# Token-major keys through DRAM instead of TensorE, a partial sum read by ScalarE, and weight pieces dealt anew, in an attention and MLP kernel

## The chip, the cores and the metric

One core of one Trainium2 chip. The metric is the device time of one execution in microseconds (us); all data are float32. Where several runs of a kernel exist, the median of its fast runs is quoted.

## The reference, cut to what matters

```python
def _attn_ref(q, k, v, f_logit):              # batch 4, 8 heads, 768 tokens, head size 48
    f = 1.0 / (1.0 + np.exp(-f_logit))
    for t in range(S):
        state = f[:, :, t, :, None] * state + np.einsum('bhd,bhe->bhde', k[:, :, t], v[:, :, t])
        y[:, :, t] = np.einsum('bhd,bhde->bhe', q[:, :, t], state)

def _moe_ref(x, w_in, w_out):                 # x: (3072, 384), d_ff = 2048
    h = x @ w_in
    g = h * (1.0 / (1.0 + np.exp(-1.702 * h)))
    return g @ w_out
```

The output y of the recurrence, transposed to (3072, 384), is the x of the MLP.

## The kernel before

The sequence is cut into 12 units of 256 tokens. In each unit the recurrence is done in six levels of blocks: masked scores of decayed keys and queries (`sc`), their products with v (`y`), then the products of keys and v that give the new states (also a bank named `sc`, told apart by its line: L523 before, L552 after), then the part of y that comes from the states of before (`inter`). Feature-major q, k and f come from VectorE's 32x32 block transposes; units 0 to 2 use TensorE for that. The MLP of earlier units is dealt in small portions between these parts, so that TensorE has something to do while the other engines prepare the next part. Weights arrive packed and are converted piece by piece in units 0 to 3.

The state products need the keys token-major (`kn`). They are turned on TensorE:

```python
        def turn_k(a0):
            if a0 == 0:
                t["kn"] = att.tile([P, NP, NG, P], F32, tag="kn", name=f"kn_{n}", bufs=1)
            pt = ps.tile([P, 2, NG, P], F32, tag="mm", name=f"tkn_{n}_{a0}", bufs=4)
            for a in range(2):
                for g in range(NG):
                    x = (a0 + a) * U + g * G
                    nc.tensor.transpose(pt[:, a, g, :], X[:, 1, x:x + G], ident)
            nc.scalar.copy(t["kn"][:, a0:a0 + 2], pt)

        for a0 in (0, 2):
            part("T")(lambda a0=a0: turn_k(a0))
```

Order of the parts, and the share of the MLP that is dealt behind each:

```python
            else:                                   # next unit's turning, units 3 and later
                kind, states = parts.pop()
                parts += [("B", begin_k), (kind, lambda: (states(), begin_gates()))]
                parts.insert(i - 3, ("B", lambda: (begin_f(), begin())))
    # ... cut ...
    def steady(kind):
        return {"W": 3, "V": 4, "S": 3, "T": 1, "B": 1, "K": 1}.get(kind, 0)
    # ... cut ... the fifth argument is the number of weight pieces converted in the unit
    merge(0, fill, 0, steady, 8)
    fill += mlp_blocks((0, 0)) + mlp_blocks((0, 1))
    merge(1, fill, UNIT // 2 - LAG // 2, steady, 10, hold=1)
    # ... cut ...
    merge(2, fill, UNIT, steady, 8)
    # ... cut ...
    merge(3, fill, 3 * UNIT // 2 - LAG // 2, steady, 6, by=0.7)
```

The second MLP product of units 3 and later is done with seven half-size products in banks X, W, Y and Z, some of which are read and then go on accumulating. Y's first reader was on VectorE:

```python
        def p6():
            nc.vector.tensor_tensor(row("u2"), t["p1"], t["Y"], ALU.add)
        def p3():
            nc.vector.tensor_tensor(out_(0)[:, HC:], t["u2"], t["Z"], ALU.add)
            store(n, 0, out_(0))
```

Of the kernel before, what the change touches and what calls it, by code (L numbers as in the profile page):

```python
# [9 lines left out]
F32 = mybir.dt.float32  # L10
# [3 lines left out]
ALU = mybir.AluOpType  # L14
# [9 lines left out]
def kernel(  # L24
# [33 lines left out]
    nc = tc.nc  # L58
    B, H, S, D = q.shape
    DM = H * D  # L60
    DFF = moe_w_in.shape[1]
    P = 128
    C = 64
    G = 128
    U = 256
    NG = U // G
    NC = U // C
    NU = S // U
    NP = H // 2
# [3 lines left out]
    NK = DM // P  # L73
    NFF = DFF // P
    FG = 4
    PAIRS_AHEAD = 3
    N_FILL = 3
    N_TURN = 2
    NA = NP * U
    NALL = B * NU  # L80
    assert S % U == 0 and NALL % 2 == 0 and NL == 6 and NG == 2 and DM % P == 0 and D <= HS

    const = ctx.enter_context(tc.tile_pool(name="const", bufs=1))
    ld = ctx.enter_context(tc.tile_pool(name="ld", bufs=1))
    att = ctx.enter_context(tc.tile_pool(name="att", bufs=1))
    wp = ctx.enter_context(tc.tile_pool(name="wp", bufs=2))
    mlp = ctx.enter_context(tc.tile_pool(name="mlp", bufs=2))
# [44 lines left out]
    X = const.tile([P, 3, NX], F32, name="X")  # L132
# [6 lines left out]

    w_in = const.tile([P, NK, DFF], F32, name="w_in")  # L140
    w_out = const.tile([P, NFF, DM], F32, name="w_out")
    v_toks = [tc.dram_tile([U, DM], F32, name=f"v_tok{j}") for j in range(2)]
    D2, DR = 2 * D, P - 2 * D
    assert NP == NK + 1 and NK * DR == D2
# [5 lines left out]
    for r in range(NGR):  # L150
        ffs = range(r * FG, (r + 1) * FG)
        for ff in ffs[::2]:
            f = slice(ff * P, (ff + 2) * P)
# [159 lines left out]
    def attention(n):  # L313
# [5 lines left out]
        t = {"tms": [F]}  # L319
        parts = []  # L320

        def part(kind):
            return lambda fn: parts.append((kind, fn))
# [174 lines left out]
# [7 lines that stand above are left out]
                    nc.tensor.transpose(pt[:, a, g, :], X[:, 1, x:x + G], ident)  # L505
            nc.scalar.copy(t["kn"][:, a0:a0 + 2], pt)

        for a0 in (0, 2):
            part("T")(lambda a0=a0: turn_k(a0))

        @part("S")
        def _():
# [139 lines left out]
    def mlp_o7(n, g):  # L652
        a = lambda i, j: lambda f: g[j * 2 + f // FG][:, f % FG, i * G:(i + 1) * G]
        s = lambda i: lambda f: g["S", f // FG][:, f % FG, i * G:(i + 1) * G]
        b = lambda i, j: lambda f: quarter(w_out, i, j)[:, f]
        T_ = lambda i: lambda f: T[i][:, f] if i < 4 else T[4](f)
        t = {}

        def out_(tt):
            if "o" not in g:  # L660
                g["o"] = mlp.tile([P, U // P, DM], F32, tag="osb", name=f"osb_{n}", bufs=1)
            return g["o"][:, tt]

        def row(name):
            t[name] = mlp.tile([P, HC], F32, tag=name, name=f"{name}_{n}", bufs=1)
            return t[name]

        def p1():
            nc.scalar.copy(row("p1"), t["X"])

        def p4():
            nc.scalar.copy(row("p4"), t["W"])

        def p2():
            nc.scalar.copy(out_(0)[:, :HC], t["X"])
            last_sum(n, g)

        def p6():
            nc.vector.tensor_tensor(row("u2"), t["p1"], t["Y"], ALU.add)  # L679

        def p5():
            nc.scalar.copy(row("p5"), t["Z"])

        def p7():
            nc.vector.tensor_tensor(row("u3"), t["p1"], t["Y"], ALU.add)
            nc.vector.tensor_tensor(out_(1)[:, :HC], t["u3"], t["p4"], ALU.subtract)
            nc.vector.tensor_tensor(out_(1)[:, HC:], t["u3"], t["p5"], ALU.add)
            store(n, 1, out_(1))

        def p3():  # L690
            nc.vector.tensor_tensor(out_(0)[:, HC:], t["u2"], t["Z"], ALU.add)
            store(n, 0, out_(0))


        products = (
            ("X", a(0, 0), b(0, 0), p1, True), ("W", a(1, 1), T_(4), p4, True), ("X", a(0, 1), b(1, 0), p2, False),
            ("Y", s(0), T_(2), p6, True), ("Z", a(1, 0), T_(1), p5, True), ("Y", s(1), T_(3), p7, False),
            ("Z", a(0, 1), b(1, 1), p3, False),
        )

        def one(bank, lhs, rhs, done, new, f):
            if new and f == 0:
                t[bank] = ps.tile([P, HC], F32, tag="mm", name=f"o_{n}_{bank}", bufs=4)
            nc.tensor.matmul(  # L704
                t[bank], lhsT=lhs(f), rhs=rhs(f), start=(new and f == 0), stop=(f == HF - 1), skip_group_check=True,
            )
            if f == HF - 1:
                done()
        return [(HC, lambda p=p, f=f: one(*p, f), 0) for p in products for f in range(HF)]
# [104 lines left out]
    def parts_of(n):  # L814

        parts = list(units[n][1])
        _, inter = parts.pop()
        if n:
            kind, scores = parts[0]
            _, ahead = units[n - 1][1][-1]  # L820
            parts[0] = kind, lambda: (ahead(), scores())
        if n < N_TURN:

            def with_v(l):
                kind, fn = parts[l]
                return kind, lambda: (fn(), load_vl(n, l) if n == 0 or l else None, keep_up(2 * (n == 0 and l < 3)))
            parts[:NL] = [with_v(l) for l in range(NL)]
        if n + 1 < NALL:
            begin_f, begin, begin_k, begin_gates = units[n + 1][0]
            i = len(parts)  # L830
            if n + 1 < N_FILL:

                parts.append(("K", lambda: (begin_k(), begin_gates(), load_vl(n + 1, 0) if n + 1 < N_TURN else None)))
                parts.insert(i - 4, ("B", begin if n == 0 else lambda: None))
                parts.insert(i - 5, ("B", begin_f))
                if n:

                    kind, head = parts[0]
                    parts[0] = kind, lambda: (head(), begin())
            else:  # L840
                kind, states = parts.pop()
                parts += [("B", begin_k), (kind, lambda: (states(), begin_gates()))]
                parts.insert(i - 3, ("B", lambda: (begin_f(), begin())))
        else:
            parts.append(("W", inter))
        return parts

    def merge(n, fill, columns, share, pieces=0, hold=0, by=1.0, chores=()):



        parts = parts_of(n)
        total = sum(share(kind) for kind, _ in parts)
        converting = {"W": 3, "T": 3, "B": 1} if n < N_FILL - 1 else {"W": 3, "V": 4, "S": 3, "T": 1, "B": 1}
        total_ops = sum(converting.get(kind, 0) for kind, _ in parts)
        held = sum(share(kind) for kind, _ in parts[:hold])
        at = at_ops = done = ops = 0
        for kind, fn in parts:
            ready = state["done"]
            fn()  # L860
            for chore in chores[:2]:
                chore()
            chores = chores[2:]
            at += share(kind)
            at_ops += converting.get(kind, 0)
            n_ops = min(int(pieces * NOP * at_ops / (by * total_ops)), pieces * NOP) - ops
            ops += n_ops
            first, n_columns = done, max(0, columns * (at - held) / (total - held) - done)

            def some(end):  # L870
                nonlocal done
                while fill and done < end and fill[0][2] <= ready:
                    w, emit, _ = fill.pop(0)
                    emit()
                    done += w
            for i in range(n_ops):
                some(first + n_columns * i / n_ops)
                convert()
            some(first + n_columns)

    def steady(kind):
        return {"W": 3, "V": 4, "S": 3, "T": 1, "B": 1, "K": 1}.get(kind, 0)

    UNIT = NFF * NK * U + U // P * NFF * DM

    for j in range(3):
# [10 lines left out]
        load_raw(1, j)  # L897
    load_vn(1)
    fill = []
    merge(0, fill, 0, steady, 8)  # L900
    fill += mlp_blocks((0, 0)) + mlp_blocks((0, 1))
    merge(1, fill, UNIT // 2 - LAG // 2, steady, 10, hold=1)
    fill += mlp_blocks((1, 0), (1, 1)) + mlp_blocks((0, 2), (1, 2))
    merge(2, fill, UNIT, steady, 8)
    fill += mlp_blocks((2, 0), (2, 1)) + mlp_blocks((2, 2), (0, 3)) + mlp_blocks((1, 3), (2, 3))
    merge(3, fill, 3 * UNIT // 2 - LAG // 2, steady, 6, by=0.7)
    fill_order.close()
    for n in range(3, NALL):
        fill += mlp_unit(n)
    for n in range(4, NALL):  # L910
        merge(n, fill, NFF * NK * U + 7 * HF * HC, steady, chores=list(sums_of_b()) if n == 4 else ())
    for _, emit, _ in fill:
        emit()

# [28 lines left out]
```

## Time and profile before

| | before |
|---|---|
| time, median of 3 runs | 658.35 us (655.55 to 660.19) |
| profiled span and its mean clock | 653.7 us, 1.000 |
| a late unit (5 to 10) | 48.71 us |
| first product of the MLP (`h`) | 51.82 us |
| first scores of unit 4 | 210.19 us |

The last line is used below as the mark between the **front** (units 0 to 3, where weights are converted) and the **late** part. The lines of the profile are in the prediction. In the rows of tenths each digit is one fortieth of the span and 9 means 90% or more. In the tables of groups and waits the name after `L` is the source line; lines of the kernel after are 2 to 31 higher.

### The profile page before, as it was taken

Reading aid. Unit: us, or ns where it says so; the run is one execution under the profiler, and the core shown is the slowest. Engines: PE = TensorE matmul, PEld = TensorE weight load, DVE = VectorE, ACT = ScalarE, POOL = GpSimd, SP = SyncE. Lnnn points to the kernel's source line nnn. Section 1 sums busy time; section 2 is a strip of 40 time slices with the busy share of each in tenths; the row PEclk is TensorE's granted clock in tenths of the full one; section 3 lists DMA queues with packets and bytes.
Section 4 is the critical chain, followed back from the end, with each engine's and each line's share of the span. In section 5 each row is a group of like instructions: output and inputs, shape, how many; then the busy total and the mean of one; then the engine's idle time right before and its main releaser. Section 6 shows DMA issues by size and latency. Waiting matters only on the chain.

```text
span 653.7 us, 20397 instructions
## 1 busy us (share of the span) xinstructions
PE 632.3 (97%) x8958; PEld 542.0 (83%) x8958; DVE 444.7 (68%) x802; ACT 229.7 (35%) x477; POOL 60.2 (9%) x116
## 2 busy tenths in 40 slices
PE   6979989999999999999999999999999999999997
PEld 5656767767778789989989989989989889989997
DVE  2998978788787658558558558558559557553571
ACT  3565444333224324324324324324334333232120
POOL 3050020010001002002002002002002002000000
PEclk9999999999999999999999999999999999999999
DMA  8898874384044634614605615605604202101000
GB/s 186 211 221 216 216 157 126 99 207 79 25 91 123 167 74 121 164 29 119 167 25 127 160 27 128 159 26 129 159 27 107 64 25 64 38 2 26 25 1 24
DMA packets 67554, 67.67 MB, mean 104 GB/s; under 512 B 30410, under 2 KB 61290, under 8 KB 67466
## 3 DMA queue, kind: packets, MB, share of 16 engines
q1 hardware_dynamic: 67466, 66.38, 40.5%
q8 instruction: 70, 1.15, 0.7%
q14 instruction: 18, 0.15, 0.1%
HBM read 56.92 MB, written 8.65 MB: 100 GB/s over the span
## 4 chain that ended last, share of the span: by engine, by line
PE 85%; DVE 8%; DMA 3%; ACT 2%; issue 1%; SPq 1%; DVEq 0%; ACTq 0%
PE h L727 37%; PE o_X L704 7%; PE o L755 7%; PE o_Y L704 7%; PE o_Z L704 7%; PE sc L384 5%; PE y L448 4%; PE o_W L704 4%; PE t L339 2%; PE y L563 2%; PE sc L523 1%; PE tkn L505 1%; DMA bits<-in_moe_w_in_dram 1%; DMA xT<-yT 1%; DVE X L439 1%
## 5 line engine op out<-in xcount | busy, mean ns | idle before, releaser
L727 PE MATMUL h<-xT,w_in 128*128 128x256 f32 (+1 forms) x1152 | 259.8, 381 | 5.7 <-DMA xT<-yT 3.0
L727 PEld LDWEIGHTS h<-xT,w_in 128*128 128x128 f32 x1152 | 215.3, 190 | 39.1 <-issue 3.8
L733 DVE TENSOR_TENSOR g<-h,sg 128x256 f32<-128x256 f32 (+1 forms) x192 | 80.8, 422 | 98.2 <-ACT sg L732 95.7
L732 ACT ACTIVATE sg<-h 128x256 f32<-128x256 f32 (+1 forms) x192 | 73.2, 383 | 193.1 <-PE h L727 186.9
L423 ACT COPY Kc<-X 128x512 f32<-128x512 f32 x69 | 46.2, 669 | 118.1 <-DVE X L439 84.7
L755 PE MATMUL o<-w_out,g 128*128 128x384 f32 x192 | 66.1, 493 | 0.0
L439 DVE TENSOR_TENSOR X<-X,tot 128x1024 f32<-128x1024 f32 x45 | 55.1, 1224 | 15.4 <-PE sc L384 10.2
L755 PEld LDWEIGHTS o<-w_out,g 128*128 128x128 f32 x192 | 35.3, 190 | 22.9 <-issue 1.4
L704 PE MATMUL o_X<-w_out,g 128*128 128x192 f32 x288 | 51.9, 329 | 0.0
L704 PE MATMUL o_Y<-T,S 128*128 128x192 f32 x288 | 51.1, 331 | 0.1
L704 PEld LDWEIGHTS o_Y<-T,S 128*128 128x128 f32 x288 | 46.5, 190 | 2.6 <-DVE u L679 1.2
L704 PEld LDWEIGHTS o_X<-w_out,g 128*128 128x128 f32 x288 | 47.3, 190 | 0.9
L410 DVE TENSOR_TENSOR A<-sc,masks 128x512 f32<-128x512 f32 x72 | 46.8, 679 | 0.0
L376 POOL TENSOR_TENSOR tot<-F 128x512 f32<-128x512 f32 x12 | 12.5, 1040 | 342.2 <-DVE st L540 342.2
L448 PE MATMUL y<-A,vl 64*48 64x64 f32 x2304 | 41.2, 217 | 0.4 <-issue 0.3
L448 PEld LDWEIGHTS y<-A,vl 64*48 64x48 f32 x2304 | 36.2, 120 | 3.9 <-issue 3.6
L327 DVE STREAM_TRANSPOSE X<-raw 128x1024 f32<-128x1024 f32 x18 | 36.7, 2040 | 2.5 <-PE y L563 2.2
L571 ACT COPY yT<-y 48x512 f32<-48x512 f32 x48 | 27.8, 580 | 13.0 <-PE y L563 12.4
L384 PEld LDWEIGHTS sc<-X,Kc 48*64 48x64 f32 x1344 | 24.0, 134 | 8.2 <-issue 3.4
L384 PE MATMUL sc<-X,Kc 48*64 48x64 f32 x1344 | 28.3, 220 | 1.8 <-DVE A L410 1.0
L376 POOL TENSOR_TENSOR tot<-tot 128x256 f32<-128x256 f32 (+4 forms) x60 | 27.4, 457 | 4.7
L704 PE MATMUL o_Z<-w_out,g 128*128 128x192 f32 x144 | 26.6, 331 | 0.0
(93 smaller groups left out, 662.5 us busy)
## 6 DMA issues: line engine op xcount, KB each, us to landing
vl<-v_tok SPq DMA_DIRECT2D x60, 192.0 KB, 2.9
bits<-in_moe_w_out_dram SPq DMA_DIRECT2D x8, 768.0 KB, 10.4
bits<-in_moe_w_in_dram SPq DMA_DIRECT2D x8, 576.0 KB, 7.0
v_tok<-in_v_dram SPq DMA_DIRECT2D x10, 384.0 KB, 4.2
vn<-v_tok SPq DMA_DIRECT2D x10, 384.0 KB, 6.9
xT<-yT SPq DMA_DIRECT2D x24, 144.0 KB, 2.8
raw<-in_q_dram SPq DMA_DIRECT2D x18, 192.0 KB, 4.0
raw<-in_f_logit_dram SPq DMA_DIRECT2D x18, 192.0 KB, 4.8
```

The costliest lines, as they stand in the source:

```text
L327: nc.vector.transpose(out.rearrange("p (a i j) -> p a j i", a=NP, j=R), raw[:, j].rearrange("p a (j d) -> p (a j) d", j=R)[:, :, :32],)
L376: nc.gpsimd.tensor_tensor(tn, t2[:, :, 0], t2[:, :, 1], ALU.mult)
L384: nc.tensor.matmul(out[g * HS:(g + 1) * HS, h, a, :], lhsT=lhs(h, a * U + g * G), rhs=rhs(h, a * U + g * G), start=True, stop=True,)
L410: nc.vector.tensor_tensor(A[:, :, c:c + w].rearrange("p h (x t) -> p h x t", t=64), t["sc"][:, :, c:c + w].rearrange("p h (x t) -> p h x t ...
L423: nc.scalar.copy(c.rearrange("p (n m) -> p n m", m=m), X[:, j, :NA].rearrange("p (n two m) -> p n two m", two=2, m=m)[:, :, hf, :],)
L439: nc.vector.tensor_tensor(qk, qk, by, ALU.mult)
L448: nc.tensor.matmul(dst(h, g, a), lhsT=vls[n, u][g * 64:(g + 1) * 64, (2 * a + h) * D:(2 * a + h + 1) * D], rhs=A(h, g, a), start=(start an ...
L704: nc.tensor.matmul(t[bank], lhsT=lhs(f), rhs=rhs(f), start=(new and f == 0), stop=(f == HF - 1), skip_group_check=True,)
L727: nc.tensor.matmul(ph, lhsT=w_in[:, c, ff * P:(ff + 1) * P], rhs=xTs[n][:, c, :], start=(c == 0), stop=(c == NK - 1))
L732: nc.scalar.activation(sg, ph, AF.Sigmoid, scale=1.702)
L733: nc.vector.tensor_tensor(g[ff // FG][:, ff % FG, :], ph, sg, ALU.mult)
L755: nc.tensor.matmul(t["po"], lhsT=g[ff // FG][:, ff % FG, tt * P:(tt + 1) * P], rhs=w_out[:, ff, :], start=(ff == ffs[0]), stop=(ff == ffs[ ...
```

## The change

Its intent: take the key transposes off TensorE, which has no gap in a late unit, and let VectorE (32x32 blocks) and a store to and fetch from DRAM (the blocks) do them for seven units, 4 to 10; put more MLP between the last scores and the states so that this detour has time; take next k behind the states; let ScalarE read the sum Y that goes on; and deal the weight pieces 6, 10, 9, 7 instead of 8, 10, 8, 6, with three `o` products' columns moved from unit 1 to unit 2.

```diff
+    CARRY = range(N_FILL + 1, NALL - 1)
...
+    k_toks = [tc.dram_tile([NG, G, P // 32, 32 * NP], F32, name=f"k_tok{j}") for j in range(2)]
...
-        for a0 in (0, 2):
-            part("T")(lambda a0=a0: turn_k(a0))
+        def carry_k(g):
+            nb = G // 32
+            z = mlp.tile([P, nb, 32, NP], F32, tag="sum", name=f"z_{n}_{g}", bufs=3)
+            nc.vector.transpose(
+                z.rearrange("p b d a -> p a b d"),
+                X[:, 1, :NA].rearrange("p (a g b t) -> p g a b t", a=NP, g=NG, b=nb)[:, g],
+            )
+            for i in range(P // 32):
+                nc.sync.dma_start(
+                    out=k_toks[n % 2][g, :, i].rearrange("(b t) x -> t b x", t=32),
+                    in_=z[i * 32:(i + 1) * 32].rearrange("p b d a -> p b (d a)"),
+                )
+
+        def fetch_k(g):
+            if g == 0:
+                t["kn"] = att.tile([P, NP, NG, P], F32, tag="kn", name=f"kn_{n}", bufs=1)
+            z = mlp.tile([P, P, NP], F32, tag="sum", name=f"kt_{n}_{g}", bufs=3)
+            nc.sync.dma_start(out=z.rearrange("p d a -> p (d a)"), in_=k_toks[n % 2][g].rearrange("t i x -> t (i x)"))
+            nc.scalar.copy(t["kn"][:, :, g, :], z.rearrange("p d a -> p a d"))
+
+        if n not in CARRY:
+            for a0 in (0, 2):
+                part("T")(lambda a0=a0: turn_k(a0))
+        else:
+            parts[-1] = "V3", parts[-1][1]
+            part("C")(lambda: (carry_k(0), fetch_k(0)))
+            part("C2")(lambda: (carry_k(1), fetch_k(1)))
...
         def p6():
-            nc.vector.tensor_tensor(row("u2"), t["p1"], t["Y"], ALU.add)
+            nc.scalar.copy(row("p6"), t["Y"])
...
-            nc.vector.tensor_tensor(out_(0)[:, HC:], t["u2"], t["Z"], ALU.add)
+            nc.vector.tensor_tensor(out_(0)[:, HC:], t["p1"], t["Z"], ALU.add)
+            nc.vector.tensor_tensor(out_(0)[:, HC:], out_(0)[:, HC:], t["p6"], ALU.add)
...
-                parts += [("B", begin_k), (kind, lambda: (states(), begin_gates()))]
-                parts.insert(i - 3, ("B", lambda: (begin_f(), begin())))
+                if n in CARRY:
+                    parts += [("B", begin_f), ("B2", begin), ("S1", lambda: (states(), begin_gates())), ("K3", begin_k)]
+                else:
+                    (as before)
...
+    def late(kind):
+        return {"V": 6, "V3": 3, "C": 2, "C2": 4, "S1": 3, "S": 5, "B": 3, "B2": 4, "K3": 3, "T": 2, "W": 5}.get(kind, 0)
...
-    merge(0, fill, 0, steady, 8)
+    merge(0, fill, 0, steady, 6)
-    merge(1, fill, UNIT // 2 - LAG // 2, steady, 10, hold=1)
+    merge(1, fill, UNIT // 2 - LAG // 2 - 3 * DM, steady, 10, hold=1)
-    merge(2, fill, UNIT, steady, 8)
+    merge(2, fill, UNIT + 3 * DM, steady, 9)
-    merge(3, fill, 3 * UNIT // 2 - LAG // 2, steady, 6, by=0.7)
+    merge(3, fill, 3 * UNIT // 2 - LAG // 2, steady, 7, by=0.7)
...
-        merge(n, fill, NFF * NK * U + 7 * HF * HC, steady, chores=...)
+        merge(n, fill, NFF * NK * U + 7 * HF * HC, late, chores=...)
```

More of the change, by code (lines that the diff above doesn't have):

```diff
@@ L841, in parts_of @@
                 kind, states = parts.pop()
-                parts += [("B", begin_k), (kind, lambda: (states(), begin_gates()))]
-                parts.insert(i - 3, ("B", lambda: (begin_f(), begin())))
+                if n in CARRY:
+                    parts += [("B", begin_f), ("B2", begin), ("S1", lambda: (states(), begin_gates())), ("K3", begin_k)]
+                else:
+                    parts += [("B", begin_k), (kind, lambda: (states(), begin_gates()))]
+                    parts.insert(i - 3, ("B", lambda: (begin_f(), begin())))
         else:
@@ L910 @@
     for n in range(4, NALL):
-        merge(n, fill, NFF * NK * U + 7 * HF * HC, steady, chores=list(sums_of_b()) if n == 4 else ())
+        merge(n, fill, NFF * NK * U + 7 * HF * HC, late, chores=list(sums_of_b()) if n == 4 else ())
     for _, emit, _ in fill:
```

## The prediction

> **What bounds the kernel now.** I read the page's busy totals and slices first, then busy time by stretch, the chain over one late unit, the groups, the waits and the DMA issues.
>
> From the page of the kernel before: busy totals, and the slices of TensorE, VectorE and DMA.
>
> ```profile
> PE 632.3 (97%) x8958; PEld 542.0 (83%) x8958; DVE 444.7 (68%) x802; ACT 229.7 (35%) x477; POOL 60.2 (9%) x116
> PE   6979989999999999999999999999999999999997
> DVE  2998978788787658558558558558559557553571
> DMA  8898874384044634614605615605604202101000
> ```
>
> TensorE is full from the fourth slice (49 us) on, with only small dents; VectorE and DMA are full only in the first five slices. So there are two stages with two bounds. Busy time by stretch shows them: columns are length, then busy time and count of TensorE, weight load, VectorE, ScalarE and GpSimd, then clock, DMA share and GB/s.
>
> ```profile
> 20.00:50.00 30.00, 24.82 (x677) 18.56 (x677) 28.72 (x65) 18.95 (x35) 10.24 (x10) 1.00 0.82 203
> 125.00:160.00 35.00, 31.37 (x450) 22.65 (x449) 30.95 (x55) 13.25 (x27) 3.75 (x8) 1.00 0.64 139
> 317.06:365.87 48.81, 48.78 (x732) 44.67 (x735) 32.76 (x53) 17.34 (x36) 4.83 (x8) 1.00 0.40 101
> 463.22:511.98 48.76, 48.76 (x732) 44.66 (x735) 32.73 (x53) 17.28 (x36) 4.58 (x8) 1.00 0.34 86
> ```
>
> In 20 to 50 us VectorE works 28.72 of 30 us: it is the bound of unit 0. A late unit lasts 48.8 us and TensorE has no gap in it; VectorE (33 us), ScalarE (17 us) and DMA (40%) all have room. There only less TensorE work, or a smaller wait inside it, makes the time shorter. The chain of the late unit shows what its time is made of (start, length, what):
>
> ```profile
> 376.48 1.09 PE sc L384 x64
> 378.47 10.56 PE h L727 x48
> 389.03 0.44 PE tkn L505 x4
> 389.46 2.59 PE h L727 x12
> 392.06 0.44 PE tkn L505 x4
> 396.78 0.92 PE sc L523 x64
> 405.73 2.80 PE o_Y L704 x16
> 411.12 2.84 PE o_Y L704 x16
> ```
>
> The key transposes (L505) take 0.44 us twice in each unit and stand squarely between products of h; they are the work that the change takes from TensorE. The second o_Y chain takes 2.84 us where 16 such products take 2.60 elsewhere.
>
> [...] So the state products L523 that wait for the keys would hold everything behind them. The trace agrees: in unit 0, L523 waited 1.3 us for the copy of the keys, and nothing behind it started meanwhile. [...] The existing 128x1024 block transposes (L327) take 2.04 us. [...] the trace's 192 KB stores land after 1.9 us[...].
>
> **The change part by part.** First the groups and issues that give the costs (mean ns of one after the comma; for DMA, KB and median us to landing).
>
> ```profile
> L327 DVE STREAM_TRANSPOSE X<-raw 128x1024 f32<-128x1024 f32 x18 | 36.7, 2040 | 2.5 <-PE y L563 2.2 <-DMA vl<-v_tok 0.2
> L506 ACT COPY kn<-tkn 128x512 f32<-128x512 f32 x24 | 14.0, 584 | 2.7 <-PE tkn L505 1.9
> L423 ACT COPY Kc<-X 128x512 f32<-128x512 f32 x69 | 46.2, 669 | 118.1 <-DVE X L439 84.7
> PEld o_Y L704 <- DVE u L679: 1.2, 4, 0.3
> vl<-v_tok SPq DMA_DIRECT2D x60, 192.0 KB, 2.9
> vn<-v_tok SPq DMA_DIRECT2D x10, 384.0 KB, 6.9
> out_dram<-osb SPq DMA_DIRECT2D x18, 192.0 KB, 1.9
> ```
>
> *1. Key transposes leave TensorE.* Seven units (4 to 10) x 2 x 0.44 us = 6.2 us, all on the path, since TensorE has no gap there. In their place, each unit gets two VectorE transposes of 128x512: half of 2.04 us each, so 2.0 us; VectorE goes to about 35 of 48 us, beside the path. ScalarE's two copies stay, reading SBUF instead of PSUM: 2 x (0.669 - 0.584) = 0.17 us. DMA gets eight stores of 64 KB and two fetches of 256 KB: 1 MB more beside some 5 MB, at 40% share. None of it is on the path by its amount.
>
> *2. The latency of the detour.* It counts only if it outlasts the MLP put between the last scores and the states. My estimate for half 0: block transpose 1.0, four issues at about 0.5 = 2.0, store landing 2 to 3, issue 0.6, fetch 3 to 4, copy 0.7: 9 to 11 us. Half 1 ends about 1 to 2 us later if its stores are issued ahead of the first fetch, and about 5 to 6 us later if they queue behind it. The keys are final some 3 us after those scores start (in the trace 376.41 and about 379), so kn is ready 13 to 21 us after them. The room: a unit deals 23,040 columns in about 39 us; the new shares are 6+6+3+2+4+3+4+3+3 = 34, and 3+2+4+3+4 = 16 of them lie between V3 and the states: 39 x 16/34 = 18.4 us, plus about 3 us of scores and sums around them: 21 us. It fits, in the worst case only just. Before, the states (396.60) came 20 us after the scores as well.
>
> *3. ScalarE reads the going o_Y.* The wait in the second o_Y and the odd 0.2 us before it come from a busy VectorE queue. A 0.31 us copy on ScalarE ends the wait sooner. The o_Y products take 5.44 to 5.67 us a unit where 5.40 is free of it; nine units give about 1.2 us. VectorE gets one 0.35 us addition more per unit off the path, but at the very end of the kernel it is on it: +0.35 us.
>
> *4. Pieces 8, 10, 8, 6 become 6, 10, 9, 7.* One weight piece costs VectorE five instructions (0.55 + 0.55 + 0.35 + 0.55 + 0.35 = 2.35 us). Two fewer in unit 0, where VectorE is the bound from 14 to 42 us: -4.7 us at most, and I count -4.4 because levels also wait on scores and copies. Nothing is paid back in unit 1 (still ten), and unit 2 has the room (VectorE 22.05 of 32 us in 93 to 125). Unit 3 begins in the stretch 125 to 160, VectorE 30.95 of 35, with 3.6 us of TensorE gaps: another piece there may cost 1 us of its 2.35.
>
> *5. 3 x 384 columns moved from unit 1 to unit 2.* They are 1,152 x 1.7 ns = 1.95 us of MLP. Before, TensorE idles some 1.8 us (91.2 to 93.0) until xT has landed; this work fills that. I count -1.5 us.
>
> *Sum:* -6.2 - 1.2 + 0.35 - 4.4 + 1.0 - 1.5 = -12.0 us. Against it +1.5 us, about 0.2 us a late unit, for new small waits of tighter places (V1 and V2 get 6.9 us of MLP instead of 8.2, and next k comes behind the states). Net -10.5: 658.35 becomes about 648, 1.6% less.
>
> **The rivals.**
> *A: the states wait for the detour.* For it: half 1 may be as late as the room is long[...]. Against: that queue stands idle from about 380 to 395 us, where the new stores fall. With 1 us lost in each of seven units the kernel would be at 653 to 655; with 2 us lost at about 660, no gain.
> *B: the front gives nothing.* If DMA (82 to 89% in the first 80 us) and not VectorE times unit 0, or unit 3 pays the pieces back, only parts 1 and 3 remain: some 653. For it: ScalarE's conversions waited 3.4 us for weights. Against: one weight pair fewer is due by then, and VectorE never stops in that stretch.
> *C: VectorE's and ScalarE's queues turn against TensorE.* Block transposes of 1 us and next k's work behind the states may delay g or the next scores; k's chain (2.0 transpose, 1.3 copies, 1.2 product, 0.7 copy) is over 5 us against 3.4 + 3.4 us of MLP and 1 us of y. If program order held, up to 1 us a unit: 654. Against: in the trace next F, q and k are taken as soon as their buffers are free, and early freeing of the keys by the block transposes only helps that.
> *D: all goes well,* waits vanish and the front gives 6 us: 644 to 645, right at 2%.
>
> **Range and chances.** The removed work (6.2 us) is nearly sure; the front (0 to -6) and new waits (0 to +7) carry the spread. That gives 642.5 to 655.5. A gain over 2% (under 645.2) asks for D; I give it 0.26. Over 2% slower asks for waits of some 3 us a unit: 0.03. The rest is within 2%.
>
> **What would show it.** Right: no tkn between h products in the late units but for unit 3 and the last; a late unit of 47.6 to 47.9 us; L523 without a wait on kn; o_Y at 5.4 us a unit; first h at about 47.4 instead of 51.8 us; no gap ahead of unit 2's h. Wrong: waits of L523 on the copy of kn of over 0.5 us a unit (A), first h still at 50 us or later, or larger gaps from 125 to 160 us (B), new waits of scores on Kc or of h on g (C).

The queue in rival A is SPq, which issues the DMAs. Its longest waits in the kernel before on TensorE and VectorE were 16.6 us (on the y products, L448) and 15.8 us (on g, L733).

## The result, and the profile after

| | before, same rounds | after |
|---|---|---|
| median of 4 fast runs | 657.59 us (655.55 to 660.19) | 649.62 us (647.16 to 651.03) |
| profiled span, mean clock | 653.7 us, 1.000 | 649.2 us, 0.991 |
| late unit (mean of four) | 48.71 us | 47.63 us |
| first `h` | 51.82 us | 49.86 us |
| first scores of unit 4 | 210.19 us | 210.97 us |
| moved by DMA | 67.67 MB | 75.03 MB |

The ratio is 0.9873 (95%: 0.9823 to 0.9922), 1.3% faster, which at a threshold of 2% counts as the same. A ratio is the mean time of one kernel's fast runs over the mean of the other's in the same rounds, so it is not quite the ratio of the medians. The profiled run of the kernel after was the slowest of its four (651.03 us), that of the kernel before one of the fastest (655.66 us), so the two profiles differ by 4.5 us only.

The late units did what was asked. Busy time by stretch, kernel after (same columns as in the prediction), for the first and the last of four late units in a row:

```profile
315.00:362.63 47.63, 47.63 (x725) 43.86 (x727) 34.66 (x54) 18.15 (x37) 4.29 (x8) 1.00 0.52 130
457.88:505.51 47.63, 47.63 (x725) 43.86 (x728) 34.66 (x54) 18.12 (x37) 4.30 (x8) 1.00 0.38 103
```

TensorE is still full, with less to do; VectorE rose to 34.66 us as worked out (35). The chain of waits over one late unit, kernel after (start, length, what):

```profile
373.95 18.33 PE h L757 x84
...
393.32 0.92 PE sc L552 x64
...
404.41 2.60 PE o_Y L734 x16
...
409.61 0.65 PE o_Y L734 x4
...
412.25 2.15 PE o_Y L734 x12
```

Where `h` was broken twice by `tkn`, it now runs through, and the states follow without a wait. The second o_Y takes 0.65 + 2.15 = 2.80 us here in two pieces round the scores, and the first 2.60: 5.40 a unit. The 0.20 us above 2.60 is no wait for VectorE: in these chains the first large products right behind scores or y products take 0.20 us longer, whatever they are (twelve o_Y 2.15 instead of 1.95 us, sixteen o_X behind the states' products 2.80). The detour itself, in the timeline of the kernel after (start, length; SPq is the queue that issues the DMAs):

```profile
375.46 1.11 DVE L515 STREAM_TRANSPOSE z<-X 128x512 f32<-128x512 f32 x1
...
376.60 2.95 SPq L520 DMA_DIRECT2D k_tok<-z  x4
...
388.71 1.14 ACT L530 COPY kn<-kt 128x512 f32<-128x512 f32 x1
...
393.13 1.10 PE L552 MATMUL sc<-vn,kn 64*64 64x48 f32 x64
```

From the first block transpose to the last copy of `kn` (389.85) it is 14.4 us; the states start 3.3 us later. One term was mis-sized without harm, in the table of groups:

```profile
L530 ACT COPY kn<-kt 128x512 f32<-128x512 f32 x14 | 16.1, 1148 | 0.4 <-DMA kt<-k_tok 0.3
```

The copy costs 1.15 us and not the 0.67 us that I took from the copies L423. It reads with a step of four elements; the copies of the same size from PSUM, which read without one (L508 of the kernel after), took 0.59 us. No run changed the step alone, so what the longer time comes from was not shown.

But the mark of unit 4 is no earlier than before, although the first `h` is 2 us earlier. The page of the kernel after, its busy totals and the slices of VectorE and of the clock (the clock's row of the kernel before is all nines):

```profile
PE 629.9 (97%) x8902; PEld 540.7 (83%) x8902; DVE 458.2 (71%) x816; ACT 236.5 (36%) x486; POOL 51.9 (8%) x116
DVE  2988968778887777687687687687677675552571
PEclk9999989989999999999999999999999999999999
```

TensorE has 56 instructions fewer, worth 6.2 us, yet its busy time fell by only 2.4 us. Two slices of the clock's row show why: TensorE ran slow there. Busy time by stretch of 2 us, kernel after; the third number from the right is the granted clock:

```profile
126.00:128.00 2.00, 0.00 (x0) 0.00 (x0) 1.92 (x3) 2.00 (x5) 0.56 (x2) 1.00 0.83 209
...
130.00:132.00 2.00, 2.00 (x6) 1.55 (x6) 0.53 (x2) 0.37 (x1) 0.00 (x0) 0.50 1.09 244
...
144.00:146.00 2.00, 2.00 (x39) 1.58 (x34) 2.00 (x5) 1.17 (x3) 1.69 (x5) 0.50 0.06 17
```

and what a halved clock does to an instruction group, from the chain of waits of the same stretch:

```profile
142.98 1.99 PE sc L386 x64
```

The same 64 scores take 1.09 us in a late unit. The kernel after has three such stretches, each some 3.4 us long (81.6 to 85.0, 129.4 to 132.8, 143.0 to 146.5); the profiled run of the kernel before has none, though TensorE idles there too (columns as above):

```profile
128.00:130.00 2.00, 1.01 (x5) 0.91 (x6) 2.00 (x5) 2.00 (x6) 0.56 (x2) 1.00 0.96 228
```

**The account of the 4.5 us of span.** At the mark the kernel after has also dealt fewer products of `h`: 141 of the kind with 256 columns are recorded before it where the kernel before has 144, and three take 1.14 us. So the front cost 0.8 + 1.1 = 1.9 us, and the late part gained 5.3 + 1.1 = 6.4 us. The latter adds up: from the first scores of unit 4 to those of unit 11 the seven units take 333.97 instead of 340.79 us, 6.8 less, and the extra 0.36 us addition stands at the end: 6.5 us. Six of the seven gain 1.09 us each; unit 4, the first of the new kind, gains only 0.3, and there TensorE waited 0.4 us for `kn`. The former is the question of most experiments below: -4.9 us was expected, +1.9 came. Three stretches at half clock can cost up to 1.7 us of work each, 5 us in all, which is an estimate from their length (half of 3.4 us).

### The profile page after: what moved, and what is told of

It is laid out like the page before. It is cut to its first block, busy times and chain, and to the rows that moved or that the text cites. A ratio compares the mean times of both kernels' runs of the same rounds, so it can differ in the third digit from the quotient of the medians.

```text
span 649.2 us, 20414 instructions
## 1 busy us (share of the span) xinstructions
PE 629.9 (97%) x8902; PEld 540.7 (83%) x8902; DVE 458.2 (71%) x816; ACT 236.5 (36%) x486; POOL 51.9 (8%) x116
## 2 busy tenths in 40 slices
DMA packets 77636, 75.03 MB, mean 116 GB/s; under 512 B 31530, under 2 KB 69578, under 8 KB 77546
## 3 DMA queue, kind: packets, MB, share of 16 engines
q8 instruction: 70, 1.15, 0.8%
## 4 chain that ended last, share of the span: by engine, by line
PE 86%; DVE 6%; DMA 3%; SPq 2%; ACT 2%; issue 1%; DVEq 0%; ACTq 0%
PE h L757 37%; PE o_X L734 8%; PE o L785 8%; PE o_Y L734 7%; PE o_Z L734 7%; PE sc L386 6%; PE y L450 4%; PE o_W L734 4%; PE y L592 2%; PE sc L552 2%; DMA bits<-in_moe_w_in_dram 1%; PE t L341 1%; DMA raw<-in_q_dram 1%; SPq L253 1%; SPq L182 1%
## 5 line engine op out<-in xcount | busy, mean ns | idle before, releaser
L757 PEld LDWEIGHTS h<-xT,w_in 128*128 128x128 f32 x1152 | 218.7, 192 | 37.6 <-issue 3.0
L763 DVE TENSOR_TENSOR g<-h,sg 128x256 f32<-128x256 f32 (+1 forms) x192 | 79.4, 420 | 72.1 <-ACT sg L762 70.5
L679 DVE TENSOR_TENSOR g<-g,S 128x512 f32<-128x512 f32 x18 | 12.4, 690 | 20.0 <-PE o_X L734 20.0
L734 PE MATMUL o_Z<-T,g 128*128 128x192 f32 x144 | 24.9, 326 | 0.0
```

Of the source, the lines that this page charges most:

```text
L734: nc.tensor.matmul(t[bank], lhsT=lhs(f), rhs=rhs(f), start=(new and f == 0), stop=(f == HF - 1), skip_group_check=True,)
L757: nc.tensor.matmul(ph, lhsT=w_in[:, c, ff * P:(ff + 1) * P], rhs=xTs[n][:, c, :], start=(c == 0), stop=(c == NK - 1))
L763: nc.vector.tensor_tensor(g[ff // FG][:, ff % FG, :], ph, sg, ALU.mult)
```

## The experiments

In each batch the kernels and the kernel before ran on the same chip; unless said otherwise ratios are against the kernel before. One run of the kernel before (2279.81 us, beside experiments 5 to 8) counts as slow and is left out. My theory after the result was: the late part is as predicted, the front is paced by TensorE rather than by VectorE, and what it does gain is lost to the halved clock. The rivals: the new queues of the late units take it (C), the states wait for the detour (A), or weights by DMA pace the front (B).

**1. carry_only: the late part alone.** The kernel after with the pieces and columns of before.

```diff
-    merge(0, fill, 0, steady, 6)
+    merge(0, fill, 0, steady, 8)
-    merge(1, fill, UNIT // 2 - LAG // 2 - 3 * DM, steady, 10, hold=1)
+    merge(1, fill, UNIT // 2 - LAG // 2, steady, 10, hold=1)
-    merge(2, fill, UNIT + 3 * DM, steady, 9)
+    merge(2, fill, UNIT, steady, 8)
-    merge(3, fill, 3 * UNIT // 2 - LAG // 2, steady, 7, by=0.7)
+    merge(3, fill, 3 * UNIT // 2 - LAG // 2, steady, 6, by=0.7)
```

> The changed kernel with the old front: pieces 8, 10, 8, 6 and no columns moved from unit 1 to unit 2. Theory: the late units keep all of the gain (47.63 us a unit instead of 48.71, about 6 to 7 us over units 4 to 10) and the front is that of the kernel before, so 651 to 652 us where before is 657.6. If it equals the changed kernel within 1 us, the front gave nothing; if it is 2 to 4 us slower than the changed kernel, the front gave that. Theory on the clock: if the granted clock stays at 1.00, the drops to half clock (three stretches of 3.4 us in the changed kernel's profile, none before) come from the new front; if it drops here too, they don't.

Measured: 649.53 us, ratio 0.9886 (0.9853 to 0.9919), late unit 47.64 us, clock of the four runs 0.993 to 1.0. The late part alone gives what the whole change gives (0.9873), and 1.5 us more than I expected. The front's new dealing has a net worth near nothing. The clock answers the other question: this profile has two halved stretches (39.6 to 43.0 and 94.2 to 97.6 us), so the old front has them too.

**2. front_only: the front alone.** The kernel before with the edit of experiment 1 turned round.

> The kernel before with only the new front (pieces 6, 10, 9, 7 and 3 x 384 columns moved from unit 1 to unit 2). Prediction's steps 4 and 5: 4.9 us less, about 652.7. Theory now: first h earlier by 2 us, unit 1 shorter by 2 more, but 1 to 3 stretches of half clock (1.7 us each) in units 1 to 3, so 654 to 657 and a granted clock of 0.991 to 0.997. Rival: clock drops belong to the detour, clock 1.00 here and 653.

Measured: 659.09 us, ratio 1.0039 (1.0000 to 1.0079); clock 0.984 to 0.992, against 0.992 to 1.0 for the kernel before in the same rounds. The expectation failed: alone, the front is not faster at all. Its profile has halved stretches at 14 to 19, 38 to 43, 52 to 57 and 130 to 136 us. So rival B's outcome came; whether by B's mechanism (weights), this run doesn't show.

**3. no_shift: the change without the 3 x 384 columns.**

```diff
-    merge(1, fill, UNIT // 2 - LAG // 2 - 3 * DM, steady, 10, hold=1)
+    merge(1, fill, UNIT // 2 - LAG // 2, steady, 10, hold=1)
-    merge(2, fill, UNIT + 3 * DM, steady, 9)
+    merge(2, fill, UNIT, steady, 9)
```

> The changed kernel without the 3 x 384 columns moved from unit 1 to unit 2 (pieces stay 6, 10, 9, 7). Theory: with this MLP back in unit 1, TensorE isn't left idle ahead of unit 1's state products, the half clock stretch at 82 us is gone, but the gap of 1 to 2 us before unit 2's h is back; within 1 us of the changed kernel. If the prediction's step 5 is right as it stood, it is 1.5 us slower.

Measured: 647.32 us, ratio 0.9860 (0.9828 to 0.9892); the profiled run's clock was 1.000. Step 5 of the prediction demanded that the kernel be slower without the shift, and it is not; by the ratios it is 0.9 to 2.1 us faster than the change in its two series, within the intervals. In the same batch it is 2.2 us below carry_only, from which it differs only in the pieces; with intervals of 0.3% each way, that 2.2 us is a likely size for the pieces and not a settled one.

Its profile and that of the kernel before make a cleaner pair, since neither has a halved stretch before the mark. From the chain of waits of no_shift, its first `h` and its mark:

```profile
48.61 1.55 PE h L757 x6
...
207.59 0.94 PE sc L386 x61
```

So with the new pieces alone the first `h` is 3.2 us earlier (51.82 before) and the mark 2.6 us earlier (210.19 before). The shift did fill the gap that it was meant for. The waits of TensorE's `h` for xT, before, after and no_shift:

```profile
PE h L727 <- DMA xT<-yT: 3.0, 2, 1.8
PE h L757 <- DMA xT<-yT: 1.2, 1, 1.2
PE h L757 <- DMA xT<-yT: 3.7, 2, 2.0
```

The second wait, ahead of unit 2's `h`, is gone in the change alone. But there TensorE now waits in unit 1, three times and 1.2 us in all (78.9 to 81.3 us), where no_shift doesn't.

**4. mlp_ahead_inter: more MLP ahead of inter in units 1 and 2.** In the change TensorE was busy for 2.10 of the 3.4 us ahead of the halved stretch at 82 us and for 2.30 of the 3.4 us ahead of that at 143 us. The idle time lay at `begin_k` and behind the states, so I dealt more MLP there.

```diff
-    merge(1, fill, UNIT // 2 - LAG // 2 - 3 * DM, steady, 10, hold=1)
+    merge(1, fill, UNIT // 2 - LAG // 2 - 3 * DM, lambda kind: 3 if kind == "K" else steady(kind), 10, hold=1)
-    merge(2, fill, UNIT + 3 * DM, steady, 9)
+    merge(2, fill, UNIT + 3 * DM, lambda kind: 5 if kind == "S" else steady(kind), 9)
```

> The changed kernel with MLP dealt differently inside units 1 and 2: more of it (about 1 us each) between the states and the products that need them, where TensorE idled ahead of both half clock stretches (at 80 and at 140 us). Theory: [...] these two stretches go, the clock is 0.997 to 1.00 and the time 646 to 647.5. Rival: the stretches are chance or come from elsewhere; then no change from 649 to 650 and a clock near 0.992.

Measured: 647.12 us, ratio 0.9853 (0.9826 to 0.9880), the mark of unit 4 at 205.79 us. Better than the change by 0.2%, within the intervals, with one halved stretch of 3.4 us (124.3 to 127.7) left in its profile. The time came as expected, the clock did not: 0.992 to 0.997, little above the change's, so the filled waits may be worth more here than the clock.

**5. warm: dummy products ahead of inter.** The three halved stretches of the change come behind 3.4 us with 1.32, 2.20 and 1.11 us of idle TensorE. If this idle time brings them, dummy products in its place should keep the clock up.

```diff
-            parts[0] = kind, lambda: (ahead(), scores())
+            parts[0] = kind, lambda: (keep_up({1: 2, 2: 3, 3: 3}.get(n, 0)), ahead(), scores())
-   ... keep_up(2 * (n == 0 and l < 3)))
+   ... keep_up(2 * (n == 0 and l < 3 or n == 1 and l == 1)))
```

> The changed kernel with dummy products (the kernel's own keep-busy products, 0.75 us each) where TensorE only waits: two ahead of unit 0's state products, two ahead of unit 1's first h, three ahead of the state products of units 1 and 2. Theory: [...] with these bridged the clock is at 0.997 or better in most runs and the time 646 to 648, although the dummies add work. Rival: the dips are chance; clock stays at 0.991 to 0.997, and the dummies make it slower by up to 3 us, 650 to 653.

Measured: 650.49 us, ratio 0.9902 (0.9851 to 0.9952). In its profile the stretches at 82 and 143 us are gone, where dummies had been put; the one at 128 to 132 us stayed. The clock rose (0.994 to 0.997), but the time did not fall: the dummies add 0.75 us each (two took 1.49 us at 23.69 us in the kernel after), and likely stand on the path (first `h` at 50.89 us; the profiles with the same front and no halved stretch ahead of it have 48.06 to 50.70, so one profile can't show it). That idling has to do with the clock is supported by the two stretches that went; the remedy is not worth it.

**6. mlp_ahead_late_f: experiment 4, and unit 3's F and q turned behind the key transposes of unit 2.** In the kernel after, `h` waits 2.2 us for a copy of `kn` in unit 2, as VectorE's and ScalarE's queues hold unit 3's turning ahead of it.

```diff
-                    parts.insert(i - 3, ("B", lambda: (begin_f(), begin())))
+                    parts.insert(i - 1 if n == 2 else i - 3, ("B", lambda: (begin_f(), begin())))
```

> As mlp_ahead_inter, and in unit 2 the turning of unit 3's gates and queries comes behind the copies of unit 2's keys. In the changed kernel h waits 2.2 us there (126 to 128 us) for the copy of the keys on ScalarE, which stands in its queue behind a sigmoid that waits for VectorE. Theory: this wait and the half clock stretch behind it go, 2 to 3 us less than mlp_ahead_inter (647.1): 644 to 645.5. Rival: the turning is only delayed and the wait comes back at unit 3's first scores: no change.

Measured: 644.66 us, ratio 0.9812 (0.9772 to 0.9853), clock 0.997 to 1.0, the mark at 206.26 us. The expectation was hit, though experiment 4 ran in another batch and the two intervals overlap. With 1.9% (at a threshold of 2%: unclear) this is the best version together with experiment 10, and it has the shift of step 5 in it.

**7. short_room: less MLP ahead of the states.** The room for the detour is cut to see what waits and how much was to spare.

```diff
-   ... "S1": 3, "S": 5, "B": 3, "B2": 4, "K3": 3, "T": 2, "W": 5}
+   ... "S1": 3, "S": 5, "B": 1, "B2": 1, "K3": 8, "T": 2, "W": 5}
```

> The changed kernel with less MLP between the last scores and the states: shares B and B2 1 and 1 instead of 3 and 4, K3 8 instead of 3, the sum the same. 5/34 of 39 us = 5.7 us of MLP goes from ahead of the states to behind them. In the changed kernel the second copy of the keys is ready 3.3 us ahead of the states in a late unit (389.85 and 393.13 us), so the theory (the detour has 3 us to spare, not more) expects a wait of 2 to 3 us ahead of the states in each of the seven units, and 14 to 20 us more in all: about 663 to 668. Rival: the detour isn't near the path; under 3 us more.

Measured: 667.14 us in one run (clock 0.987). The waits of TensorE, with us in total, times and the longest:

```profile
PE sc L552 <- ACT kn L530: 11.3, 7, 7.3
```

and a piece of its chain of waits:

```profile
346.58 1.76 DMA k_tok<-z
...
348.43 3.99 DMA kt<-k_tok
...
352.44 1.13 ACT kn L530
```

Seven waits, one in each unit of the new kind: 7.3 us in unit 4, and 0.4 to 1.3 us in the six others, not the 2 to 3 us that I expected. Here the chain leaves TensorE for the detour: the last store (64 KB) lands in 1.8 us, the fetch (256 KB) in 4.0. The unit of this chain takes 49.19 us instead of 47.63, the six others 48.5 on average. Unit 4 alone takes 58.0 us, with 10.2 us at half clock from within its wait on (249.0 to 259.3 us), so that the total was hit is partly luck. But rival A's mechanism is real, and the shares as chosen stand clear of it by the 3.3 us seen above.

**8. pieces_4: four pieces in unit 0, twelve in unit 1.** If VectorE paced unit 0, two fewer pieces would gain as much again.

```diff
-    merge(0, fill, 0, steady, 6)
+    merge(0, fill, 0, steady, 4)
-   ... steady, 10, hold=1)
+   ... steady, 12, hold=1)
```

> The changed kernel with 4 pieces in unit 0 and 12 in unit 1 instead of 6 and 10. Prediction's step 4 (VectorE bounds unit 0): the levels of unit 0 come 0.5 us earlier each and first h another 4 us earlier, at 45.5 us. Theory now: the levels' pace (3.36 to 3.6 us) is set by TensorE's own chain (scores, sums, v and transposes of the next unit, dummies), so levels three to six start where they do with 6 and 8 pieces (25.1, 28.7, 32.3 us), and first h comes at most 1.5 us earlier.

Measured: 651.38 us in one run (clock 0.991), first `h` at 46.69 us. That is 3.2 us sooner than the change's profile and 1.4 to 4.0 us sooner than the profiles with six pieces and no halved stretch ahead of `h`, so likely more than I expected; but the mark of unit 4 is at 211.38, so it is given back. The levels themselves tell which engine paces. The chain of waits in unit 0, kernel before, one level:

```profile
22.50 0.62 DVE X L436
...
23.70 0.60 DVE A L410
```

the same in the kernel after:

```profile
25.18 0.62 PE sc L386 x32
...
27.05 1.75 PE t L341 x32
28.79 0.62 PE sc L386 x32
```

and in pieces_4:

```profile
24.51 0.62 PE sc L386 x32
...
28.12 0.62 PE sc L386 x32
```

In the kernel before the chain runs through VectorE's promotions and masks; in the kernel after, and in pieces_4, from about 21.7 to 34 us it runs through TensorE alone. (In no_shift, with the front pieces of the change, it runs through VectorE again, from 22.5 to 40 us.) A level takes 3.61 us in both: scores, y, the turning of v and 32 transposes of the next unit's inputs. The kernel before's fifth and sixth levels start 3.66 us apart (28.75 and 32.41 us). With 8, 6 or 4 pieces the pace is the same, so VectorE and TensorE were level there, and taking work from the busier one gained only what lies outside the levels: from the start of the sixth level to the first scores of unit 1 the kernel before takes 12.3 us, the kernel after 10.0, no_shift 9.5 and pieces_4 8.1.

**9. after_again: the change once more, five rounds.** No edit; another chip.

> The changed kernel unaltered, for a closer interval and for how often the clock drops: 647 to 651 us, ratio 0.985 to 0.989 of before; runs at clock 0.997 near 647 and runs at 0.991 near 650.5, that is some 1.7 us for each stretch of 3.4 us at half clock.

Measured: 650.96 us, ratio 0.9892 (0.9860 to 0.9923), clock 0.989 to 0.997. The result repeats.

**10. best2: experiment 6 without the shift.**

```diff
-    merge(1, fill, UNIT // 2 - LAG // 2 - 3 * DM, lambda kind: ..., 10, hold=1)
+    merge(1, fill, UNIT // 2 - LAG // 2, lambda kind: ..., 10, hold=1)
-    merge(2, fill, UNIT + 3 * DM, lambda kind: ..., 9)
+    merge(2, fill, UNIT, lambda kind: ..., 9)
```

> mlp_ahead_late_f without the 3 x 384 columns moved from unit 1 to unit 2: the best of what was found, put together. Theory: the columns moved took MLP away where TensorE waited for unit 1's states, so 0 to 2 us less than mlp_ahead_late_f (644.7), a ratio of 0.978 to 0.982. Rival: with more MLP between the states and their products the move no longer matters; 644 to 645.5 with the gap ahead of unit 2's h back.

Measured: 645.23 us, ratio 0.9817 (0.9788 to 0.9846). No better than experiment 6. At a threshold of 2% it is unclear as well. Once the waits of units 1 and 2 are mended, the shift is worth nothing that these runs resolve, so its harm in the change as made isn't a fixed cost of 1,152 columns.

**11. late_f_before: the late turning alone, in the kernel before.** The edit of experiment 6.

> The kernel before with one thing altered: in unit 2 the turning of unit 3's gates and queries comes behind the copies of unit 2's keys. There h waited 1.3 us for that copy (129 us). Theory: this wait goes and nothing else, 1 to 2 us less, 655. Rival: it was worth more in the changed kernel only with the shares altered; no change.

Measured: 660.39 us, ratio 1.0043 (1.0010 to 1.0075). A miss. The waits of TensorE for the states' updates, first the kernel before, then this one:

```profile
PE y L563 <- DVE st L543: 1.2, 3, 0.5
```

```profile
PE y L563 <- DVE st L543: 3.9, 2, 3.5
```

The wait has moved: VectorE does unit 3's turning after the keys, and now the states' updates stand behind it, 3.5 us in one place, with 6.8 us at half clock beside it (141.1 to 148.0 us). With more MLP behind the states (the share 5 of experiment 4) that wait is not there in experiment 6, so its gain belongs to the two edits together.

**12. p6_only: ScalarE reads Y, alone, in the kernel before.**

```diff
-            nc.vector.tensor_tensor(row("u2"), t["p1"], t["Y"], ALU.add)
+            nc.scalar.copy(row("p6"), t["Y"])
-            nc.vector.tensor_tensor(out_(0)[:, HC:], t["u2"], t["Z"], ALU.add)
+            nc.vector.tensor_tensor(out_(0)[:, HC:], t["p1"], t["Z"], ALU.add)
+            nc.vector.tensor_tensor(out_(0)[:, HC:], out_(0)[:, HC:], t["p6"], ALU.add)
```

> The kernel before with only ScalarE reading the o_Y that goes on. Prediction's step 3: o_Y comes down from 5.44 to 5.67 us a late unit to 5.4 us or less, nine units give 1.2 us, less 0.35 us at the end: 0.9 us, a ratio of 0.9987 that the interval may not tell from 1; the chain of the late units (48.55 to 48.81 us before) decides: 48.5 us.

Measured: 656.85 us, ratio 0.9976 (0.9950 to 1.0003), a late unit of 48.50 instead of 48.71 us. Its second o_Y, in the chain of waits:

```profile
316.48 2.60 PE o_Y L705 x16
```

where the prediction's chain had 2.84. The step is confirmed by its place; its total of 0.6 us (1.6 by the ratio) is at the edge of what the runs resolve. The first o_Y, right behind scores, still takes 2.80 us although ScalarE now reads Y: that 0.20 us was not VectorE's.

**The clock over all runs.** Each run lists its mean granted clock. Over 76 fast runs of all these kernels, compared within each kernel, 0.001 of clock goes with 0.50 us of time (correlation -0.76). The means: kernel before 0.9965, change 0.9934, front_only 0.988, carry_only 0.9965, no_shift 0.9972, experiment 6 0.9982. Carried to a clock of 1.0 with that slope, an estimate, the kernel before stands at 655.4 us, front_only at 653.1, carry_only at 647.7, the change at 646.8, experiment 6 at 643.9. By this estimate the front is worth some 1 to 2 us at equal clock and its extra halved stretches take that back. Runs at a clock of 1.000 need no slope: the kernel before at 655.46 us (median of five), carry_only at 648.10 and no_shift at 645.74 (one run each), so 7.4 us for the late part and 2.4 for the pieces.

**What the halved stretches follow.** In the kernel after, TensorE was busy for 2.10, 1.22 and 2.30 us of the 3.4 us ahead of its three halved stretches (78.18 to 81.60, 125.97 to 129.39 and 139.63 to 143.04 us). But in the kernel before it was busy for 1.64 of the 3.4 us from 89.6 to 93.0 us and for 2.08 from 126.5 to 129.9 us, in best2 for 1.86 of the 4 us from 130 to 134 us, and the clock stayed at 1.00 there and in the 2 us behind. So a wait of some 2 us can have half clock behind it or not: the same wait of 2.2 us ahead of unit 2's `h` has it in the change and not in no_shift. What else decides was not shown. One place follows the edit: a halved stretch near 130 us (124 to 135) is in all seven profiles that have the shift and not the late turning, and in none of the four with neither (before, carry_only, no_shift, p6_only).

## Why the prediction was right or wrong

The time (648.0 against 649.62 us) and the range were right, and so was the class. The sum was right partly by luck: the late part, counted at 5.6 us after new waits, gave 7.1 (from the mark to the end 443.5 us before, 436.4 in carry_only and no_shift), and the front, counted at 4.9, gave little or nothing.

- **Step 1, the key transposes: right.** 0.88 us a unit, 6.2 us in all, and nothing came in their place: a late unit fell by 1.08 us, which is 0.88 and the 0.21 of step 3. VectorE rose to 34.66 us beside the path.
- **Step 2, the latency: right, with one term mis-sized.** Half 0 was ready 9.7 us after the first block transpose, where 9 to 11 were expected, half 1 14.4 us after it, and the states came 3.3 us later. The copy cost 1.15 instead of 0.67 us, off the path. Only the first unit of the new kind waited (0.4 us). Experiment 7 shows that rival A's wait does come when the room is cut.
- **Step 3, ScalarE reads Y: right, with one reading wrong.** o_Y is 5.40 us a unit; alone the step takes 0.21 us off a late unit (experiment 12), and the extra 0.36 us addition is at the end. The "odd 0.2 us" was not a wait for VectorE; it stays, and goes to whatever comes behind the scores.
- **Step 4, "I count -4.4" for the pieces: right in direction, mis-sized, its reason half wrong.** The step that failed is "VectorE is the bound from 14 to 42 us". In the levels, 21 to 34 us, VectorE was busy, but TensorE's own program of a level takes 3.6 us as well, and the pace did not move with 8, 6 or 4 pieces; the gain lies behind the levels. A busy share of 96% showed a busy engine, not the only one. The first `h` came at 49.86 and not at 47.4 us, but another run of the same kernel has it at 51.67 and others with the same front as early as 48.06. In the pair without halved stretches the pieces are worth 2.6 us at the mark, of -4.4 + 1.0 = -3.4 forecast.
- **Step 5, "I count -1.5" for the columns: wrong.** The gap ahead of unit 2's `h` was filled, as it says; what failed is that nothing was to be paid for it. The mark is 3.4 us later than in no_shift: unit 1 waits 1.2 us more, and halved stretches come at 82, 129 and 143 us. With the waits mended it makes no difference (experiment 10).
- **The +1.0 us of unit 3 and the +1.5 us of small waits: not found as such.** The late units had no new waits except unit 4's. In their place stood what I had no term for, the halved clock, which the profile of before could not show because that run had none.
- **Rivals.** A: not in the change, shown by force in experiment 7. B, "the front gives nothing": its outcome came (the mark at 210.97 us, experiments 1 and 2). Its mechanism, weights by DMA, isn't what the chain shows in the levels, but it isn't excluded: behind the levels the chain of the kernel before runs through a weight load (29.5 to 37.3 us), that of after_again too (26.6 to 34.0 us), and no run changed the loads alone. C: no new wait of scores or of `h` in the late units. D asked for all to go well; experiment 6 reaches its 644 to 645 us with two more edits.

So where did the front's expected gain go? Of the pieces' part most came, 2.6 of 3.4 us. The shift took that back, by new waits and by halved stretches. That the stretches follow idle time is supported by experiments 5 and 6, in which mending the idle place removed stretches: in 5 those at 82 and 143 us, in 6 the one near 130 us, though the profile of 6 has one at 75.2 to 78.6 us. But in the kernel before 1.76 us of idle TensorE in 3.4 us (89.6 to 93.0) left the clock at 1.00, so what makes a wait halve the clock was not shown, and no run controlled the stretches one by one. How much of the 3.4 us is due to them and how much to the waits themselves stays open; the 0.50 us per 0.001 is a slope, not a test.

## What to carry to other kernels

A transpose through DRAM was a good trade here, where TensorE has no gaps and the result is needed late: it took 14 us of latency that the MLP covers and gave back all its TensorE time. Before taking work from a busy engine, work out the other engines' program for the same stretch; when two are level, taking from one gives only what lies outside their stretch. And when a kernel idles in its front, compare the granted clock of several runs before reading a difference of 2 to 3 us as worth of an edit: the change ran in 647.16 us at 0.997 and in 653.12 at 0.992.
